# Exchanging the head of a fused attention and feed-forward kernel: single x tiles before the weights, chunk 0 in halves, dummy matmuls, V copied in one instruction

## Chip, cores and metric

One core of a Trainium2 chip runs the whole program. The time is device microseconds of one execution; lower is better. Five engines work side by side, each through its own instruction list in a fixed order: PE (matrix products), DVE (vector), ACT (scalar functions), POOL (general purpose) and SP, which here only starts transfers. An instruction that must wait for another engine or for a transfer holds up everything behind it on its own engine.

## What is computed

A transformer layer on x of 2048 rows (tokens) and 448 columns, bfloat16, cut to what matters:

```python
def layer(x):                       # x: 2048 x 448
    n = layernorm(x)
    q = n @ wq                      # 16 heads of 28
    k, v = n @ wk, n @ wv           # one head of 28, shared by all 16
    o = softmax(q @ k.T * 28**-0.5) @ v
    h = x + o @ wo
    n2 = layernorm(h)
    r = n2 @ w_r                    # pick the 8 best rows by r
    y = (silu(n2[idx] @ w_gate) * (n2[idx] @ w_up)) @ w_down * sigmoid(r[idx])
    return h + n2 + scatter(y, idx)
```

## The kernel before

**Tiles.** The 2048 tokens are 16 tiles of 128 (`t`, `j`), four of which make a chunk of 512. Attention runs in 16 blocks: block `b` is four heads (group `g = b % 4`) by the 512 queries of chunk `b // 4`. For each block and each of the 16 key tiles there are two products of Q with K (`qk`, one for each pair `p` of heads, into two banks of PSUM), an exponential of each on ACT (`act_unit`, L753, 128 x 1024 values), and four products with V that add up in bank 6 or 7 (`act_pv`). In blocks 1 to 15 three or four of the 16 key tiles go past ACT: `dve_unit` and `shift` build an approximate exponential on DVE out of integers (tile Y, L766 and L772, through PSUM banks 4 and 5, three Y buffers), and `dve_pv` multiplies its four shifted copies with four scaled copies of V. Block 0 has no such tile: all its 32 exponentials are ACT's.

**The head.** Before the first exponential there must be Q of block 0 and K of the first key tiles. `chunk(c)` makes K and V for 512 tokens: statistics (`bn_stats`, `bn_aggr`, L464 and L466) and normalisation (L479) of four tiles on DVE, rstd by Ln and Exp on ACT for chunk 0 and by a power on POOL for the others, transposes on PE, copies to `xnT` (L490 on ACT, L493 on DVE), the K product, K written twice with scale and offset (L501 on ACT, L505 on DVE), the V product, and five scaled copies of V (L516 on DVE). `q_project(b)` makes Q of a block (copied by L456). `wk_rep`, `wq_pad` and `wv_pad` are the weights spread out to 32 columns a head with zeros between, by POOL. All chunks but the first go through one PSUM bank, number 7 (`MISC`).

**Loads.** SP issues them in order: x tiles 0-1, 2-3, wk, wq, wv, the rest of x in fours, then w_r, the three feed-forward weights and wo.

**The order.** It isn't written out. Every operation is entered with its engine, its cost in ns, what it reads and writes, and a priority (lower first). `_Graph.plan` walks through time with these costs: an engine that is free takes, of the operations that are ready, the one of lowest priority, and ties go to the one entered first; if none is ready it takes the one that becomes ready next. After an operation its results count as ready only after `LAT` (190 ns PE, 110 ACT, 90 DVE, 120 POOL) and `SEM` (70 ns), after a transfer only after its `lat`. The order that comes out of this is fixed for each engine; on the chip, each engine follows it, however long things really take. Reading and writing a PSUM bank counts as using the key `pk(bank)`, so two operations on one bank run in the order in which they were entered. Events are entered by time: `chunk(c)` at 4c - 9, a tile of block b at 16b + j or so. So all chunks are entered before the first Y tile of block 1, which stands at 16.5.

Of the kernel before, what the change touches and what calls it, by code (L numbers as in the profile page):

```python
# [230 lines left out]
def _main(nc, G, sb, ps, psb, flag, scr, xs, A_x, A_wq, A_wk, A_wv, A_wo, B_w_r, B_w_gate, B_w_up, B_w_down, out,  # L231
          exact=False):
    S, D, H, C = A_x.shape[1], A_x.shape[2], 16, 8
    DH = D // H
# [10 lines left out]
    VC = (1.0, 1.6796875, 1.4140625, 1.1875, 1.0)  # L245
# [25 lines left out]
    vone = sb("vone", [128, NV, 4, 32], F32)  # L271
# [119 lines left out]
    G.op(PO, lambda e: e.memset(wk_rep[:, :, :], 0.0), 530, writes=["wk_rep"])  # L391
    for i in range(4):
        G.op(PO, lambda e, i=i: e.tensor_copy(wk_rep[0:CK, :, 32 * i:32 * i + DH], wk_sb[0:CK, :, :]), 300,
             reads=["wk_sb"], writes=["wk_rep"])
    G.op(PO, lambda e: e.memset(wq_pad[:, :, :, :], 0.0), 1800, writes=["wq_pad"])
    for ch in range(NCH):
        v = wq_pad[0:CK, ch, :, :].rearrange("p g (i c) -> p (g i) c", c=32)[:, :, 0:DH]
        G.op(PO, lambda e, ch=ch, v=v: e.tensor_copy(v, wq_sb[0:CK, ch, :].rearrange("p (h d) -> p h d", d=DH)), 590,
             reads=["wq_sb"], writes=["wq_pad"])
    G.op(PO, lambda e: e.memset(wv_pad[:, :, :], 0.0), 210, writes=["wv_pad"])  # L400
    G.op(PO, lambda e: e.tensor_copy(wv_pad[0:CK, :, 1:1 + DH], wv_sb[0:CK, :, :]), 280,
         reads=["wv_sb"], writes=["wv_pad"])
    G.op(PO, lambda e: e.memset(vone[:, :, :, :], 0.0), 500, writes=["vone"])
# [32 lines left out]
    G.op(DV, lambda e: e.memset(Lmx[:, :], 1.0), 90, writes=["Lmx"])  # L436
    G.op(DV, lambda e: e.tensor_reduce(sw[:, 0:1], w_rb[:, :], AX.X, ALU.add), dvt(D), reads=["w_rb"], writes=["sw"])
    G.op(DV, lambda e: e.tensor_scalar(sw[:, 1:2], sw[:, 0:1], -1.0, None, ALU.mult), 70, reads=["sw"], writes=["nsw"])

    head_banks = [7, 6, 5, 4, 3, 2, 1, 0]  # L440
    hb = [0]

    def head_bank(c):
        if c > 0:
            return MISC
        b = head_banks[hb[0] % len(head_banks)]
        hb[0] += 1
        return b
# [10 lines left out]
    def chunk(c):  # L459
# [48 lines left out]
        if c == 0:  # L508
            q_project(0, head_bank(c))
# [520 lines left out]
```

## Time and profile before

| | us |
|---|---|
| runs | 426.35, 428.45, 427.67 |
| median | 427.67 |
| profiled execution | 429.03 |
| its span, first to last instruction | 427.6 |

| engine | busy us | share | instructions |
|---|---|---|---|
| PE, products | 353.3 | 83% | 3243 |
| PE, weight loads | 106.0 | 25% | 3243 |
| DVE | 363.0 | 85% | 792 |
| ACT | 380.6 | 89% | 425 |
| POOL | 50.6 | 12% | 76 |

How to read the lines that follow. Engine rows of the 40 slices give the busy share in tenths, a slice being 10.7 us; PEclk is the granted clock of PE in tenths. The chain of waits gives the shares of the span on the way back from the last instruction. A group reads: line, engine, operation, written tile <- read tile, shapes, count | busy us in total, mean ns of one | idle us of the engine just before them and who ended it. In order of time a row reads: start, duration, engine, line, operation, count, and in brackets the idle time before it and what ended it. A windows row reads: from:to, length, then busy us and count for PE, its weight loads, DVE, ACT and POOL, granted clock, DMA share and GB/s (with one line of the kernel chosen, only the engine of that line has busy time). A row of DMA issues gives the count, the size of one in KB and the us from issue to landing. For a single tile a row gives duration in ns as least/median/most, and first and last start in us. SPq is SP's own instruction that issues a transfer.

### The profile page before, as it was taken

The page shows a single profiled execution, that of the slowest core. Times are in us where ns is not written, and L with a number is a line of the kernel's source. Part 1 is how long each engine was busy: PE and PEld are TensorE (multiplying, and loading weights), DVE is VectorE, ACT ScalarE, POOL GpSimd, SP SyncE. Part 2 cuts the span into 40 slices and gives each one's busy share as a digit, 9 for nine tenths or more (in the row PEclk, how much of TensorE's full clock was granted, in tenths as well). Part 3 has the DMA queues.
Part 4 walks back from the last instruction along what each step waited for, and adds up shares of the span by engine and source line. Part 5 has one row for each costly group of instructions (what it writes and reads, how often), then busy time and mean ns, then how long its engine had stood idle before and what let it go on. Part 6 is the DMA issues. An engine that isn't in the chain of part 4 may idle for free.

```text
span 427.6 us, 7935 instructions
## 1 busy us (share of the span) xinstructions
PE 353.3 (83%) x3243; PEld 106.0 (25%) x3243; DVE 363.0 (85%) x792; ACT 380.6 (89%) x425; POOL 50.6 (12%) x76
## 2 busy tenths in 40 slices
PE   0887898887888899789898897989898997898754
PEld 0333212221222222222222222222222222222243
DVE  4999819989897889989988999898989999998361
ACT  1397699999999999999999999999999999999640
POOL 8210000010010112010101030010101120313000
PEclk9998859999999999999999999999999999999965
DMA  8960000000000000200000001200000002000010
GB/s 225 266 206 19 2 2 28 2 27 2 26 3 20 10 17 12 90 25 3 27 2 26 4 25 53 63 0 26 6 27 2 18 10 91 27 2 27 2 44 8
DMA packets 17350, 15.75 MB, mean 37 GB/s; under 512 B 5944, under 2 KB 14428, under 8 KB 17308
## 3 DMA queue, kind: packets, MB, share of 16 engines
q1 hardware_dynamic: 17212, 15.16, 12.1%
q8 instruction: 27, 0.44, 0.4%
q14 instruction: 15, 0.12, 0.1%
q0 software_dynamic: 96, 0.02, 0.0%
HBM read 11.70 MB, written 3.47 MB: 35 GB/s over the span
## 4 chain that ended last, share of the span: by engine, by line
ACT 56%; PE 22%; DVE 18%; DMA 1%; issue 1%; SPq 1%; POOL 0%; POOLq 0%; DVEq 0%
ACT P L753 55%; PE ps L349 22%; DVE Y L766 5%; DVE Y L772 4%; DMA x_sb<-in_A_x_dram 1%; DVE xn L479 1%; DVE Ot L551 1%; DVE bn L464 1%; DVE K L505 1%; DVE xnT L493 1%; DVE Vs L516 1%; SPq L363 1%; DVE bn L687 1%; DVE junk L656 1%; DVE junk L664 0%
## 5 line engine op out<-in xcount | busy, mean ns | idle before, releaser
L753 ACT ACTIVATE P<-ps 128x1024 bf16<-128x1024 f32 x398 | 369.3, 1107 | 14.2 <-PE ps L349 12.8
L349 PE MATMUL ps<-Q,K 64*128 64x512 bf16 x1024 | 185.6, 391 | 44.0 <-ACT P L753 29.6
L766 DVE TENSOR_SCALAR Y<-ps 128x512 int16<-128x512 f32 x228 | 147.4, 682 | 18.0 <-PE ps L349 18.0
L772 DVE TENSOR_SCALAR Y<-Y 128x2048 int16<-128x2048 int16 x171 | 116.0, 710 | 1.4
L349 PEld LDWEIGHTS ps<-Q,K 64*128 64x128 bf16 x1024 | 44.7, 93 | 194.6 <-ACT P L753 156.1
L349 PE MATMUL ps<-P,Vs 128*32 128x512 bf16 x796 | 80.8, 396 | 0.3 <-ACT P L753 0.3
L349 PE MATMUL ps<-Y,Vs 128*32 128x512 bf16 x912 | 74.3, 383 | 0.0
L563 POOL TENSOR_TENSOR On<-Ot,Rb 128x512 bf16<-128x512 f32 x15 | 22.5, 1498 | 247.9 <-DMA Rb<-l_scr 247.9
L349 PEld LDWEIGHTS ps<-P,Vs 128*32 128x32 bf16 x796 | 20.5, 93 | 49.3 <-issue 48.3
L349 PEld LDWEIGHTS ps<-Y,Vs 128*32 128x32 bf16 x912 | 23.1, 96 | 18.4 <-issue 8.9
L349 PE MATMUL ps<-xnT,wq_pad 112*128 112x512 bf16 x64 | 21.8, 437 | 1.6 <-DVE Ot L551 1.3
L349 PE MATMUL ps<-wo_pad,On 128*128 128x448 bf16 (+1 forms) x64 | 17.8, 358 | 1.9 <-DVE Ot L551 1.1
L585 POOL TENSOR_TENSOR st<-st,nhalf 128x1 f32<-128x1 f32 x12 | 10.1, 841 | 65.8 <-DVE st L583 65.8
L456 DVE TENSOR_SCALAR Q<-ps,qone 128x512 bf16<-128x512 f32 x16 | 11.7, 732 | 7.0 <-PE ps L349 6.9
L551 DVE COPY Ot<-ps 128x512 f32<-128x512 f32 x15 | 10.3, 689 | 6.8 <-PE ps L349 6.1
L352 PE MATMUL ps<-ident,xn 128*112 128x128 bf16 x64 | 6.3, 259 | 11.2 <-POOL vone L405 10.5
L464 DVE BATCH_NORM_STATS2 bn<-x_sb 128x6 f32<-128x448 bf16 x16 | 9.4, 606 | 4.4 <-DMA x_sb<-in_A_x_dram 4.4
L579 DVE TENSOR_TENSOR hbuf<-ps,x_sb 128x448 f32<-128x448 f32 x12 | 7.5, 621 | 2.5 <-PE ps L349 2.5
L352 PEld LDWEIGHTS ps<-ident,xn 128*112 128x112 bf16 x64 | 5.2, 161 | 13.3 <-POOL vone L405 10.5
L598 DVE SCALAR_TENSOR_TENSOR junk<-hbuf,st,w_rb 128x448 bf16<-128x448 f32 x12 | 8.1, 678 | 0.0
L581 DVE BATCH_NORM_STATS2 bn<-hbuf 128x6 f32<-128x448 f32 x12 | 7.5, 622 | 0.1
L349 PEld LDWEIGHTS ps<-xnT,wq_pad 112*128 112x128 bf16 x64 | 4.4, 104 | 12.4 <-issue 8.1
(164 smaller groups left out, 156.7 us busy)
## 6 DMA issues: line engine op xcount, KB each, us to landing
Rb<-l_scr SPq DMA_DIRECT2D x15, 256.0 KB
wg_sb<-in_B_w_gate_dram SPq DMA_DIRECT2D x1, 1568.0 KB, 11.5
wu_sb<-in_B_w_up_dram SPq DMA_DIRECT2D x1, 1568.0 KB, 17.0
wd_sb<-in_B_w_down_dram SPq DMA_DIRECT2D x1, 1568.0 KB, 21.2
x_sb<-in_A_x_dram SPq DMA_DIRECT2D x3, 448.0 KB, 6.4
out_dram<-x_sb SPq DMA_DIRECT2D x3, 448.0 KB, 2.8
xn_scr<-xn SPq DMA_DIRECT2D x3, 448.0 KB, 3.8
x_sb<-in_A_x_dram SPq DMA_DIRECT2D x2, 224.0 KB, 2.8
```

Of the source, the lines that this page charges most:

```text
L349: return lambda e: e.matmul(o, lhsT=l, rhs=r, start=start, stop=stop)
L352: return lambda e: e.transpose(o, i, ident[0:p, 0:p])
L456: G.op(DV, lambda e: e.tensor_scalar(Q[:, b % 4, :], ps[:, bank, :], qone[:, 0:1], None, ALU.add), dvt(512), reads=[pk(bank), "qone"], wri ...
L464: G.op(DV, [lambda e, t=t: e.bn_stats(bn6[:, t, :], x_sb[:, t, 0:D])], dvt(D), reads=[("x", t)], writes=[("bn6", t)])
L551: G.op(DV, lambda e: e.tensor_copy(Ot[:, rb, :], ps[:, acc_bank(b), :]), dvt(512), reads=[pk(acc_bank(b))], writes=[("Ot", rb)], prio=u - 30)
L563: G.op(PO, lambda e: e.tensor_tensor(On[:, qb % 2, g, :], Ot[:, rb, :], Rb[:, rb, :], ALU.mult), 1270, reads=[("Ot", rb), ("Rb", rb)], wri ...
L579: G.op(DV, lambda e: e.tensor_tensor(hbuf[:, hr, :], ps[:, bank, 0:D], x_sb[:, t, 0:D], ALU.add), dvt(D), reads=[pk(bank), ("x", t)], writ ...
L585: G.op(PO, lambda e: e.tensor_tensor(st[:, t, 4:5], st[:, t, 7:8], nhalf[:, 0:1], ALU.pow), 570, reads=[("st7", t), "nhalf"], writes=[("st ...
L598: G.op(DV, lambda e: e.scalar_tensor_tensor(junk[:, :], hbuf[:, hr, :], st[:, t, 4:5], w_rb[:, :], ALU.mult, ALU.mult, accum_out=st[:, t, ...
L753: G.op(AC, lambda e: e.activation(P[:, sl, :, :], ps[:, b0:b0 + 2, :], ACT.Exp, bias=EBIAS, scale=OCT), 905, reads=[pk(b0), pk(b0 + 1)], w ...
L766: G.op(DV, lambda e, k=k: e.tensor_scalar(Y[:, n, 0, p + 2 * k, :].bitcast(I16), ps[:, 4 + k, :], 0.0, 32639.0 - 3 * STEP, ALU.max, ALU.mi ...
L772: G.op(DV, lambda e: e.tensor_scalar(Y[:, n, v, :, :].bitcast(I16), Y[:, n, 0, :, :].bitcast(I16), v * STEP, None, ALU.add), 610, reads=[( ...
```

## The change

- x tiles 0 to 3 are loaded one by one, then wk, wv, wq; the rest of x waits until tile 3 has landed; wo, w_r and the feed-forward weights wait until x tile 15 has landed. wo's four transfers no longer wait for one another.
- The weights are spread by ACT (`wk_rep` in one instruction, `wv_pad`, two of four pieces of `wq_pad`) and POOL (the other two). The zeros of `wk_rep` and `wv_pad` are written by DVE.
- Chunk 0 (`chunk0`, new): 44 dummy products of `ident` with itself into bank 7 first; rstd by halves of two tiles; transposes by tile into banks 0 to 3; the first half's `xnT` copied by ACT, the second's by DVE; K and Q of chunk 0 by halves of 256 tokens, K written by ACT; Q of the first half by ACT, of the second by DVE. Q of block 1 is entered at priority 9 instead of -100.
- Chunks 1 to 3: rstd of chunk 1 on ACT; five of twelve normalisations on POOL (with a negated mean, `nmean`); banks 7, 4, 5 in rotation in place of bank 7 alone. Statistics of a chunk wait for the last tile's statistics of the chunk before.
- V: the four scaled copies (five before, two of which had the scale 1.0) are written by one DVE instruction with a broadcast, and the column of constants is set once by POOL.
- `sw`, the sum over w_r, moves to priority 20.

```diff
-    VC = (1.0, 1.6796875, 1.4140625, 1.1875, 1.0)
+    VC = (1.0, 1.6796875, 1.4140625, 1.1875)
...
-    dma(x_sb[:, 0:2, 0:D], x_v[:, 0:2, :], [("x", t) for t in range(0, 2)], lat=2600.0)
-    dma(x_sb[:, 2:4, 0:D], x_v[:, 2:4, :], [("x", t) for t in range(2, 4)], lat=2600.0)
+    for t in range(4):
+        dma(x_sb[:, t, 0:D], x_v[:, t, :], [("x", t)], lat=2700.0 + 250 * t)
     dma(wk_sb[0:CK, :, :], A_wk.rearrange("(k p) n -> p k n", p=CK), ["wk_sb"], lat=4000.0)
-    dma(wq_sb[0:CK, :, :], A_wq.rearrange("(k p) n -> p k n", p=CK), ["wq_sb"], lat=6000.0)
-    dma(wv_sb[0:CK, :, :], A_wv.rearrange("(k p) n -> p k n", p=CK), ["wv_sb"], lat=6500.0)
+    dma(wv_sb[0:CK, :, :], A_wv.rearrange("(k p) n -> p k n", p=CK), ["wv_sb"], lat=4000.0)
+    dma(wq_sb[0:CK, :, :], A_wq.rearrange("(k p) n -> p k n", p=CK), ["wq_sb"], lat=5500.0)
     for i in range(4, NT, 4):
-        dma(x_sb[:, i:i + 4, 0:D], x_v[:, i:i + 4, :], [("x", t) for t in range(i, i + 4)], lat=6000.0)
+        dma(x_sb[:, i:i + 4, 0:D], x_v[:, i:i + 4, :], [("x", t) for t in range(i, i + 4)], lat=3500.0 + 400 * i,
+            reads=[("x", 3)])
...
+        if ch % 2:
+            G.op(AC, lambda e, v=v, w=w: e.activation(v, w, ACT.Identity), 480, reads=["wq_sb", "wq_pad"],
+                 writes=[("wq_pad", ch)])
+        else:
+            G.op(PO, lambda e, v=v, w=w: e.tensor_copy(v, w), 590, reads=["wq_sb", "wq_pad"],
+                 writes=[("wq_pad", ch)])
...
+    def v_project(c, bank):
+        pv = ps[:, bank, 0:128].rearrange("p (t c) -> p t c", c=32)
...
+        G.op(DV, lambda e: e.tensor_tensor(Vs[:, :, 4 * c:4 * c + 4, 1:32],
+                                           pv[:, :, 1:32].unsqueeze(1).broadcast_to([128, NV, 4, 31]),
+                                           vcc[:, :].unsqueeze(2).unsqueeze(3).broadcast_to([128, NV, 4, 31]),
+                                           ALU.mult), 620, reads=[pk(bank), "vcc"], writes=[("V", c)])
+
+    def chunk0():
+        G.prio = -500
+        for _ in range(44):
+            G.op(PE, mm(ps[:, 7, 0:128], ident[:, :], ident[:, :], True, True), 107, reads=["ident"], writes=[pk(7)],
+                 prio=-900)
...
+                G.op(AC, lambda e, sl=sl: e.activation(rstd[:, sl], var[:, sl], ACT.Exp, scale=-0.5), 200,
+                     reads=[("var", t // 2)], writes=[("rstd", -1 - t // 2)])
...
+            for kind in (("K", "Q") if h == 0 else ("Q", "K")):
+                bank = (4 if kind == "K" else 6) + h
...
+        v_project(0, 5)
+        G.prio = 9
+        q_project(1, MISC)
...
+        def head_bank():
+            hb[0] += 1
+            return (7, 4, 5)[hb[0] % 3]
...
-        for v in range(NV):
-            G.op(DV, lambda e, pv=pv, c=c, v=v: e.scalar_tensor_tensor(Vs[:, v, 4 * c:4 * c + 4, :], pv, VC[v],
-                                                                       vone[:, v, :, :], ALU.mult, ALU.add),
-                 dvt(128), reads=[pk(bank), "vone"], writes=[("V", c, v)])
+        v_project(c, head_bank())
...
-        G.op(PE, [mm(ps[32 * i:32 * i + 32, acc_bank(b), :], Vs[:, v + 1, j, :], Y[:, n, v, i, :], f, l)
+        G.op(PE, [mm(ps[32 * i:32 * i + 32, acc_bank(b), :], Vs[:, (v + 1) % NV, j, :], Y[:, n, v, i, :], f, l)
```

More of the change, by code (lines that the diff above doesn't have):

```diff
@@ L390, in _main @@
          writes=["qone"])
[L391 to L394, printed above, removed]
     G.op(PO, lambda e: e.memset(wq_pad[:, :, :, :], 0.0), 1800, writes=["wq_pad"])
+    G.op(DV, lambda e: e.memset(wk_rep[:, :, :], 0.0), 300, writes=["wk_rep"])
+    G.op(DV, lambda e: e.memset(wv_pad[:, :, :], 0.0), 100, writes=["wv_pad"])
@@ L400, in _main @@
[L400 to L403, printed above, removed]
+        w = wq_sb[0:CK, ch, :].rearrange("p (h d) -> p h d", d=DH)
+        if ch % 2:
[4 more added lines that the diff above has]
+                 writes=[("wq_pad", ch)])
@@ L577, in out_proj @@
                       for g in range(g2, g2 + 2)], 2 * 200,
-                 reads=[("On", qb % 2, g) for g in range(4)] + ["wo_pad"], writes=[pk(bank)])
+                 reads=[("On", qb % 2, g) for g in range(4)] + ["wo_pad"] + wok, writes=[pk(bank)])
         G.op(DV, lambda e: e.tensor_tensor(hbuf[:, hr, :], ps[:, bank, 0:D], x_sb[:, t, 0:D], ALU.add), dvt(D),
@@ L615, in first_top @@
         first_row(bank)
-    old = [("xnT", 0), ("xnT", 1)]
+    old = xk(0) + xk(1)
     def first_row(bank):
```

199 lines of the change are left out of this document (122 added, 77 removed).

## The prediction

> **What bounds the kernel now.** I read the page first: engine shares, the 40 slices, the chain of waits.
>
> ```profile
> span 427.6 us, 7935 instructions
> ACT  1397699999999999999999999999999999999640
> PEclk9998859999999999999999999999999999999965
> ACT P L753 55%; PE ps L349 22%; DVE Y L766 5%; DVE Y L772 4%; DMA x_sb<-in_A_x_dram 1%; DVE xn L479 1%; DVE Ot L551 1%; DVE bn L464 1%; DVE K L505 1%; DVE xnT L493 1%; DVE Vs L516 1%; SPq L363 1%; DVE bn L687 1%; DVE junk L656 1%; DVE junk L664 0%
> L753 ACT ACTIVATE P<-ps 128x1024 bf16<-128x1024 f32 x398 | 369.3, 1107 | 14.2 <-PE ps L349 12.8
> ```
>
> The 398 exponentials of L753 on ACT are the bound, except in the first six slices. So I split their time by windows, and listed ACT in order of time.
>
> ```profile
> 0.00:19.69 19.69, 0.00 (x0) 1.00 0.93 244
> 19.69:64.72 45.03, 35.74 (x37) 0.81 0.22 64
> 64.72:393.00 328.28, 326.80 (x355) 1.00 0.07 23
> 38.01 1.02 ACT L753 ACTIVATE P<-ps 128x1024 bf16<-128x1024 f32 x1 [2.11 <-PE ps L349]
> 48.97 1.02 ACT L753 ACTIVATE P<-ps 128x1024 bf16<-128x1024 f32 x1 [1.83 <-PE ps L349]
> 53.47 7.58 ACT L753 ACTIVATE P<-ps 128x1024 bf16<-128x1024 f32 x8 [1.32 <-PE ps L349]
> 61.85 2.12 ACT L753 ACTIVATE P<-ps 128x1024 bf16<-128x1024 f32 x2 [0.81 <-PE ps L349]
> 64.72 37.16 ACT L753 ACTIVATE P<-ps 128x1024 bf16<-128x1024 f32 x40 [0.75 <-PE ps L349]
> ```
>
> From 64.72 us on, 355 exponentials take 328.28 us, 0.925 each: nothing to win there, and the change leaves that part alone. The head loses twice. The first exponential starts at 19.69. The next 37 take 45.03 us where 37 x 0.925 = 34.2 would do: **10.8 us of waits**. The long ones, 2.11 and 1.83, are for the K of chunks 2 and 3 (16 keys of 128 make 32 exponentials per block; a chunk of K feeds 8).
>
> Why K is late, by engine:
>
> ```profile
> 20.00:51.00 31.00, 24.06 (x223) 9.85 (x221) 30.83 (x74) 24.67 (x26) 2.02 (x2) 0.93 0.30 90
> 51.00:63.50 12.50, 11.76 (x54) 2.23 (x54) 1.44 (x2) 10.29 (x12) 0.00 (x0) 0.50 0.01 1
> L766 DVE TENSOR_SCALAR Y<-ps 128x512 int16<-128x512 f32 x13 | 8.6, 687 | 3.3 <-PE ps L349 3.3
> L772 DVE TENSOR_SCALAR Y<-Y 128x2048 int16<-128x2048 int16 x9 | 6.0, 690 | 0.0
> 8.93 0.63 DVE L464 BATCH_NORM_STATS2 bn<-x_sb 128x6 f32<-128x448 bf16 x1 [2.69 <-DMA x_sb<-in_A_x_dram]
> ```
>
> DVE (third busy figure) is full for 31 us, then works 1.44 us of 12.5. In the full stretch it makes block 1's Y tiles (L766 and L772, 12 and 9 of the instructions) while ACT waits for chunks 2 and 3. The planner's fixed order let them in because all of chunks 1 to 3 pass through one bank. The last row is the same fault earlier: chunk 1's statistics were ordered ahead of chunk 0's normalisation, and DVE stood 2.69 us for their load.
>
> **The change, part by part.** The order on each engine follows from the costs in the diff; I walked `plan` through by hand for the head. Where an instruction stands comes from there, how long it lasts from rows.
>
> **First exponential.** It hangs on wq:
>
> ```profile
> 0.72 0.95 SPq L363 DMA_DIRECT2D x_sb<-in_A_x_dram  x2
> 2.23 0.48 SPq L363 DMA_DIRECT2D wq_sb<-in_A_wq_dram  x1
> 2.76 0.49 SPq L363 DMA_DIRECT2D wv_sb<-in_A_wv_dram  x1
> wq_sb<-in_A_wq_dram SPq DMA_DIRECT2D x1, 392.0 KB, 5.2
> L398 POOL COPY wq_pad<-wq_sb 112x448 bf16<-112x448 bf16 x4 | 2.3, 572 | 0.7 <-DMA wq_sb<-in_A_wq_dram 0.7
> 6.27 0.20 ACT L471 ACTIVATE var<-var 128x4 f32<-128x4 f32 x1 [4.27 <-DVE var L468]
> 11.66 1.02 ACT L490 ACTIVATE xnT<-ps 112x1024 bf16<-112x1024 bf16 x1 [4.95 <-PE ps L352]
> 15.53 0.78 ACT L501 ACTIVATE K<-ps,kb,ksc 128x512 bf16<-128x512 f32 x1 [2.85 <-PE ps L349]
> 13.62 1.86 PE L349 MATMUL ps<-xnT,wk_rep 112*128 112x512 bf16 x4 [1.15 <-DVE mv L466]
> 17.46 1.87 PE L349 MATMUL ps<-xnT,wq_pad 112*128 112x512 bf16 x4
> 19.26 0.75 PE L349 MATMUL ps<-Q,K 64*128 64x512 bf16 x4
> 25.09 1.04 PE L349 MATMUL ps<-xnT,wk_rep 112*128 112x512 bf16 x4
> ```
>
> wq lands at 2.23 + 5.2 = 7.4 now. Two more issues of x (0.48 each) and wv's (0.49) move ahead of its own: 1.45 later if issuing decides, about 0 if bytes do (25 KB more). I take 7.8, near the bytes, since its 5.2 us are mostly other data ahead of it. Bounds 7.4 to 8.9.
>
> In the plan wq is due at 5.92 and the second half's rstd (`Exp`) at 5.96, so on ACT two wq_pad copies stand ahead of that Exp and of the xnT copies; all of these wait in order for wq. From 7.8: two copies at 0.55 (POOL's 572 ns; ACT does not show them) make 8.9, Exp 0.2 makes 9.1, two half xnT at 0.6 (of 1.02) make 10.3. The K matmul of half 0 is half of 1.86 at the slow clock: 11.4 with its latency. Then ACT writes K twice and Q once at 0.45 (between 0.20 for 4 and 0.78 for 512): 12.8. PE meanwhile runs Q, Q, K of 0.85 each to 13.9, ACT writes the second K half, and the first exponential starts at **15.0**: 4.7 us earlier. ACT has nothing else to do before that; DVE's and POOL's chunk-0 steps end sooner and cost nothing. With PE fast the four half matmuls save 1.5.
>
> The rows show PE slow from 13.62 until the 0.75 at 19.26 (1.04 for the same four matmuls later), 5.6 us of steady work. The 44 dummies end near 6.6 (44 x 107 ns as the diff costs them); the gap to the first K matmul at 10.4 holds only transposes, so I take PE as slow. The Trainium skill, "TensorE: Matmul & The Clock Gate", Part 1 (The HAM clock gate), says that some 3.4 us of steady matmuls lift the gate and an idle window of 3.4 us brings it down. The row's 5.6 us is longer than its first figure; its second speaks against the dummies as placed, since their gap is 3.8 us. By lifting alone the estimate for the total would be 1.5 us lower; by both halves it is unchanged.
>
> **K of chunk 1.** Its matmul uses bank 7 after block 1's Q projection, whose DVE copy stands ahead of chunk 1's last `bn_aggr` (12.48 against 12.57 in the plan). Counting from Q's second half at 13.5 with the rows below: statistics and V to 15.6, Q of block 1 off PE at 17.0 and copied by 17.8, Ln and Exp between exponentials to 19.4, normalised at 20.4, transposed and copied at 22.2, K matmul 23.4, K at 24.2, exponential at 24.7. ACT is through with chunk 0 at 15.0 + 8 x 0.925 + 0.45 for Ln and Exp = 22.8: **a wait of 1.9**.
>
> ```profile
> L479 DVE TENSOR_SCALAR xn<-x_sb,mv,rstd 128x448 bf16<-128x448 bf16 x12 | 4.0, 394 | 0.0
> L493 DVE COPY xnT<-ps 112x1024 bf16<-112x1024 bf16 x6 | 4.1, 687 | 0.0
> L505 DVE TENSOR_SCALAR K<-ps,ksc,kb 128x512 bf16<-128x512 f32 x6 | 4.6, 802 | 0.0
> L579 DVE TENSOR_TENSOR hbuf<-ps,x_sb 128x448 f32<-128x448 f32 x12 | 7.5, 621 | 2.5 <-PE ps L349 2.5
> 49.85 1.08 DVE L516 SCALAR_TENSOR_TENSOR Vs<-ps,vone 128x128 bf16<-128x128 f32 x5
> L563 POOL TENSOR_TENSOR On<-Ot,Rb x15: 1267/1275/3502, 73.8 to 390.2; 128x512 bf16<-128x512 f32 x15
> ```
>
> **K of chunks 2 and 3.** Banks 7, 4, 5 now rotate, and Y uses 4 and 5. Y's instructions come later in the program, so no Y tile can start before chunk 3's K is written: DVE does chunks first. The V copy in one instruction of 496 elements is nearest to L579's 621 ns for 448; 0.6 for 1.08, 0.4 saved a chunk. Five normalisations go to POOL: bounds 0.57 (L398, one input) and 3.5 (longest of L563), taken 0.9. A mean of DVE's rows holds about 0.08 of overlap with the next instruction, so a chunk costs it four statistics at 0.6, two or three normalisations at 0.33, two copies at 0.6, two K at 0.72 and V's 0.6: some 6.5 us. Chunk 2's statistics are done while chunk 1 waits for POOL and PE, so after K1's second half at 25.0 come V, two normalisations, transposes and copies (1.9), K matmul (1.2) and K: K2 near 30, K3 one chunk later near 37. They are needed 8 x 0.925 = 7.4 apart, at 32.1 and 39.5: no wait. The Trainium skill, "GPSIMD Engine Reference", section 8 (Key points), has POOL share its SBUF interfaces with DVE; L563's spread of 1.27 to 3.50 agrees. At 3.5 each and 1.0 for each rstd, chunks 2 and 3 would cost POOL 16 us from 21 on, and with 2.7 for transposes, matmul and K the last K would come near 40, 0.5 late.
>
> **What stays.** Waits at 53.47, 61.85 and 64.72 fall in the stretch of clock 0.50; block 0 without Y's matmuls loads PE as lightly as then, so I keep all 2.88, 3.3 with a semaphore's hop each. The weights that now load after x have no reader before block 1 ends, and their 4.8 MB cross while no other load is due; without that cover the block's Rb loads would queue behind them. `sw`'s reduction moves behind the chunks into DVE's free time.
>
> **Sum.** 4.7 earlier; waits 0.45 + 1.9 + 3.3 = 5.65 instead of 10.8, 5.15 less; together 9.85. The profiled execution took 429.03 (span 427.6 and 1.4 around it): 419.2. The median shown, 427.67, lies 1.36 lower, so **417.8**.
>
> **Rivals.**
>
> 1. PE stays fast through chunk 0 and the late waits shrink too: first exponential at 13.5 and waits of about 3. 14 us, 413.7. For it: 25.09's speed and chunk work through 33 us; against: the gap after the dummies.
>
> 2. The waits come back: the order misses its loads as it did at 8.93, DVE stands for chunk 1, and all 10.8 stay. Only the earlier start counts, 4.7: 423.0. For it: wq is due at 5.92 in the plan and lands near 7.8; against: every late step is late by about the same 2 us.
>
> 3. Slower: PE holds its slow clock through block 0. These rows are the pattern:
>
> ```profile
> 56.00:58.00 2.00, 1.86 (x10) 0.32 (x8) 0.00 (x0) 2.00 (x3) 0.00 (x0) 0.50 0.00 0
> 41.09 1.10 PE L352 MATMUL ps<-ident,xn 128*112 128x128 bf16 x8
> 57.47 0.61 PE L349 MATMUL ps<-Q,K 64*128 64x512 bf16 x2
> ```
>
> At clock 0.50 the exponentials' own matmuls fill PE (1.86 of 2) and just feed ACT. Everything else then waits in ACT's time: three chunks of 2 x 1.10 + 1.86 + 0.6, three Q projections of 1.87, six Y products of 0.61, 23 us in all. With 0.45 that makes 12.65 more waits than the 10.8, less 4.7: 435.6. It decides from 15.5 us of waits on, two thirds of that work done slow. Against: PE came back to speed at 19.26 after 5.6 us of full work.
>
> 4. The head does not do what it says, nothing moves at the end: 427.7.
>
> **How the numbers follow.** Forecast 0.58, rival 1 0.15, rival 2 0.17, rival 3 0.07, rival 4 0.03. About 0.5% (2 us) is what a measurement here can tell from no change. Faster by more: 0.58 + 0.15 + 0.16 = 0.89; within: 0.04; slower: 0.07. The range runs from beyond rival 1 (wq at its early bound 7.4 on top, and its waits down by 0.8: 412.5) to just past rival 2 (423.5).
>
> **What would show it.** First exponential near 15.0; on ACT before it wq_pad copies waiting on wq's DMA near 7.8; no L766 before chunk 3's K; DVE's Q copy of block 1 ahead of `bn_aggr`; one wait of about 2 before the ninth exponential; the 40-exponential run starting near 55 instead of 64.72. It is wrong if the clock reads 0.50 for most of 20 to 45 us, if ACT waits more than 3 us for chunk 2 or 3, or if waits appear after block 1.

## The result, and the profile after

| | before | after |
|---|---|---|
| median, us | 428.06 (426.35 to 429.75, 4 runs) | 416.74 (415.54 to 417.05, 4 runs) |
| profiled execution, its span, us | 429.03, 427.6 | 416.59, 414.6 |
| first exponential starts, us | 19.69 | 15.02 |
| 38th exponential starts, us | 64.7 | 53.6 |
| waits between them, us | 10.8 | 4.4 |
| last exponential ends, us | 399.83 | 388.67 |

The ratio is 0.973 with an interval of 0.9686 to 0.9775: 11.3 us between the medians, where 9.85 were forecast. All of it is there by the 38th exponential (64.7 to 53.6, 11.1 earlier) and stays the same to the last one (11.16). In this table and below, the start of the 38th is the start of the run of exponentials in which it stands plus 0.925 for each one ahead of it in that run, and the waits are what is left of the way from the first to the 38th after 37 x 0.925 = 34.2. The traces' own start of the 38th lies within 0.4 of this figure.

The page after: span, the rows of ACT and of the granted clock in the 40 slices (10.4 us each now), and the group of exponentials.

```profile
span 414.6 us, 8038 instructions
ACT  4779999999999999999999999999999999999640
PEclk9799999999999999999999999999999999999955
L823 ACT ACTIVATE P<-ps 128x1024 bf16<-128x1024 f32 x398 | 368.5, 1116 | 5.1 <-PE ps L350 3.9
```

ACT is at 9 from the fourth slice on, where before it was from the sixth, and the granted clock has lost its dip (8, 8 and 5 in slices four to six); a 7 stands in the second slice, chunk 0's. The same 398 exponentials of the same length now stand idle 5.1 us in all, 14.2 before.

ACT in order of time:

```profile
7.74 1.04 ACT L405 ACTIVATE wq_pad<-wq_sb 112x448 bf16<-112x448 bf16 x2 [1.06 <-DMA wq_sb<-in_A_wq_dram]
...
8.78 1.06 ACT L501 ACTIVATE xnT<-ps 112x512 bf16<-112x512 bf16 x2
11.55 1.02 ACT L525 ACTIVATE K<-ps,kb,ksc 128x256 bf16<-128x256 f32 x2 [1.70 <-PE ps L350]
...
14.11 1.02 ACT L525 ACTIVATE K<-ps,kb,ksc 128x256 bf16<-128x256 f32 x2 [1.18 <-PE ps L350]
15.02 1.94 ACT L823 ACTIVATE P<-ps 128x1024 bf16<-128x1024 f32 x2
...
20.51 2.87 ACT L823 ACTIVATE P<-ps 128x1024 bf16<-128x1024 f32 x3 [0.53 <-PE ps L350]
25.14 4.93 ACT L823 ACTIVATE P<-ps 128x1024 bf16<-128x1024 f32 x5 [1.76 <-PE ps L350]
30.40 5.72 ACT L823 ACTIVATE P<-ps 128x1024 bf16<-128x1024 f32 x6 [0.34 <-PE ps L350]
36.55 2.86 ACT L823 ACTIVATE P<-ps 128x1024 bf16<-128x1024 f32 x3 [0.43 <-PE ps L350]
39.75 70.72 ACT L823 ACTIVATE P<-ps 128x1024 bf16<-128x1024 f32 x77 [0.34 <-PE ps L350]
```

The wait of 1.76 stands ahead of the ninth exponential: it is for chunk 1's K. Those for the K of chunks 2 and 3, 2.11 and 1.83 before, are gone, and so are the waits of 1.32, 0.81 and 0.75 at 53 to 65 us: from 39.75 on, 77 exponentials run without a listed stop, to the end of the view at 110 us.

DVE in order of time, the rows that tell the order:

```profile
21.38 0.72 DVE L463 TENSOR_SCALAR Q<-ps,qone 128x512 bf16<-128x512 f32 x1
...
23.86 1.51 DVE L588 TENSOR_SCALAR K<-ps,ksc,kb 128x512 bf16<-128x512 f32 x2
...
35.89 1.53 DVE L588 TENSOR_SCALAR K<-ps,ksc,kb 128x512 bf16<-128x512 f32 x2
...
38.53 1.29 DVE L836 TENSOR_SCALAR Y<-ps 128x512 int16<-128x512 f32 x2
```

The first Y tile starts after chunk 3's K, as forecast. Block 1's Q is copied at 21.38, much later than forecast: see below.

### The profile page after: what moved, and what is told of

Its sections match the earlier page's. It is cut to its first block, busy times and chain, and to the rows that moved or that the text cites. A ratio compares the mean times of both kernels' runs of the same rounds, so it can differ in the third digit from the quotient of the medians.

```text
span 414.6 us, 8038 instructions
## 1 busy us (share of the span) xinstructions
PE 349.3 (84%) x3295; PEld 110.5 (27%) x3295; DVE 359.5 (87%) x774; ACT 383.3 (92%) x438; POOL 49.5 (12%) x73
## 3 DMA queue, kind: packets, MB, share of 16 engines
q1 hardware_dynamic: 17244, 15.16, 13.3%
## 4 chain that ended last, share of the span: by engine, by line
ACT 62%; PE 21%; DVE 12%; DMA 2%; issue 1%; SPq 1%; POOL 0%; POOLq 0%; DVEq 0%; ACTq 0%
ACT P L823 62%; PE ps L350 21%; DVE Y L836 2%; DVE Y L842 1%; DVE K L588 1%; DVE Ot L621 1%; DMA wq_sb<-in_A_wq_dram 1%; DVE xnT L581 1%; DMA Lc<-l_scr 1%; SPq L364 1%; DVE bn L547 1%; DMA l_scr<-Ot 1%; DVE xn L565 1%; DVE junk L726 1%; DVE bn L757 1%
## 5 line engine op out<-in xcount | busy, mean ns | idle before, releaser
L350 PE MATMUL ps<-Q,K 64*128 64x512 bf16 x1024 | 182.7, 386 | 45.9 <-ACT P L823 32.3
L836 DVE TENSOR_SCALAR Y<-ps 128x512 int16<-128x512 f32 x228 | 147.2, 682 | 13.9 <-PE ps L350 13.8
L842 DVE TENSOR_SCALAR Y<-Y 128x2048 int16<-128x2048 int16 x171 | 114.7, 705 | 1.6
L350 PE MATMUL ps<-P,Vs 128*32 128x512 bf16 x796 | 79.3, 389 | 0.0
L633 POOL TENSOR_TENSOR On<-Ot,Rb 128x512 bf16<-128x512 f32 x15 | 21.4, 1429 | 239.4 <-DMA Rb<-l_scr 239.4
L350 PE MATMUL ps<-xnT,wq_pad 112*128 112x512 bf16 (+1 forms) x68 | 20.1, 393 | 0.6 <-DVE Ot L621 0.6
L350 PE MATMUL ps<-wo_pad,On 128*128 128x448 bf16 (+1 forms) x64 | 17.8, 358 | 2.3 <-DVE Ot L621 1.5
L621 DVE COPY Ot<-ps 128x512 f32<-128x512 f32 x15 | 10.3, 689 | 0.9 <-PE ps L350 0.3
L353 PE MATMUL ps<-ident,xn 128*112 128x128 bf16 x64 | 5.3, 236 | 3.1 <-DVE xn L493 2.7
L350 PEld LDWEIGHTS ps<-wo_pad,On 128*128 128x128 bf16 x64 | 4.2, 97 | 11.7 <-issue 6.9
L547 DVE BATCH_NORM_STATS2 bn<-x_sb 128x6 f32<-128x448 bf16 x12 | 6.9, 605 | 0.0
```

The source lines that it names most:

```text
L350: return lambda e: e.matmul(o, lhsT=l, rhs=r, start=start, stop=stop)
L547: G.op(DV, [lambda e, t=t: e.bn_stats(bn6[:, t, :], x_sb[:, t, 0:D])], 540, reads=[("x", t), ("mv", 4 * c - 1)], writes=[("bn6", t)])
L621: G.op(DV, lambda e: e.tensor_copy(Ot[:, rb, :], ps[:, acc_bank(b), :]), dvt(512), reads=[pk(acc_bank(b))], writes=[("Ot", rb)], prio=u - 30)
L633: G.op(PO, lambda e: e.tensor_tensor(On[:, qb % 2, g, :], Ot[:, rb, :], Rb[:, rb, :], ALU.mult), 1270, reads=[("Ot", rb), ("Rb", rb)], wri ...
L836: G.op(DV, lambda e, k=k: e.tensor_scalar(Y[:, n, 0, p + 2 * k, :].bitcast(I16), ps[:, 4 + k, :], 0.0, 32639.0 - 3 * STEP, ALU.max, ALU.mi ...
L842: G.op(DV, lambda e: e.tensor_scalar(Y[:, n, v, :, :].bitcast(I16), Y[:, n, 0, :, :].bitcast(I16), v * STEP, None, ALU.add), 610, reads=[( ...
```

## The experiments

The theory after the result: the gain has three sources that add up, the earlier first exponential, the bank rotation (chunks 1 to 3 ahead of the Y tiles), and a PE clock that no longer falls. The rivals: dummy products, POOL's normalisations or V's single instruction carry it; or it is the bank alone, or the order alone.

| run | first exponential | 38th | waits | median (range), us | ratio to before, 95% |
|---|---|---|---|---|---|
| e1_no_dummies | 15.00 | 53.5 | 4.3 | 416.52 (416.46 to 417.88) | 0.9655 to 0.9768 |
| e2_one_bank | 14.72 | 59.6 | 10.7 | 423.15 (421.91 to 424.83) | 0.9791 to 0.9918 |
| e3_before_rotate | 18.86 | 59.4 | 6.3 | 422.79 (421.31 to 423.51) | 0.9777 to 0.9894 |
| e4_wq_due | 12.93 | 50.6 | 3.4 | 413.00 (412.76 to 413.22) | 0.9565 to 0.9673 |
| e5_one_bank_hold | 15.16 | 56.4 | 7.1 | 420.63 (417.98 to 420.91) | 0.9722 to 0.9803 |
| e6_due_no_dummies | 13.75 | 51.4 | 3.4 | 414.46 (414.06 to 415.73) | 0.9619 to 0.9675 |
| e7_due_q1 | 13.61 | 53.1 | 5.3 | 416.62 (415.83 to 418.05) | 0.9657 to 0.9706 |
| e8_v_four | 14.98 | 53.9 | 4.7 | 416.47 (414.85 to 418.09) | 0.9689 to 0.9763 |
| e9_xn_dve | 14.59 | 52.2 | 3.4 | 415.69 (414.66 to 416.57) | 0.9677 to 0.9744 |
| e10_loads_free | 16.67 | 74.0 | 23.1 | 436.54 (435.47 to 437.70) | 1.0119 to 1.0185 |
| e11_due_v_late | 12.19 | 50.0 | 3.6 | 413.13 (412.22 to 413.81) | 0.9616 to 0.9680 |
| e12_due_xn_dve | 13.08 | 51.0 | 3.7 | 414.29 (412.99 to 415.67) | 0.9645 to 0.9735 |

The median of before beside them was 429.87 (e1 to e4), 429.72 (e5, e6, e7, e10), 427.97 (e8, e9, e11) and 427.99 (e12).

### The rotation of banks: undone, and alone

In the changed kernel, bank 7 alone again for chunks 1 to 3:

```diff
         def head_bank():
             hb[0] += 1
-            return (7, 4, 5)[hb[0] % 3]
+            return MISC
```

> The changed kernel with chunks 1 to 3 through bank 7 alone, as before. Theory: the bank rotation is what keeps block 1's Y tiles behind the chunks; with it gone the Y tiles stand among them in DVE's order again, ACT waits for K of chunks 2 and 3 (2 us or more each) and PE's clock may fall to 0.50 once more; the waits up to the 38th exponential grow from 4.3 to 8 to 11 us, 420.5 to 423.5. First exponential unchanged at 15.0. Rival: the waits shrank because DVE has less to do (POOL's normalisations, V in one instruction, ACT's share of chunk 0); then under 1.5 us is lost, 416.7 to 418.2.

In the kernel before, the rotation for chunks 1 to 3 and nothing else:

```diff
+    hc = [0]
...
-            return MISC
+            hc[0] += 1
+            return (7, 4, 5)[hc[0] % 3]
```

> The kernel before, with only the rotation of banks 7, 4, 5 for chunks 1 to 3 put in. Theory: first exponential stays at 19.7, no Y tile before chunk 3's K, the waits up to the 38th exponential fall from 10.8 to 4 to 6 us: 421.5 to 425. Rival: without the lighter DVE load of the new head K of chunks 2 and 3 is as late as before: no faster than 426.5.

ACT with one bank, in order of time:

```profile
27.86 1.02 ACT L823 ACTIVATE P<-ps 128x1024 bf16<-128x1024 f32 x1 [4.66 <-PE ps L350]
...
45.30 1.02 ACT L823 ACTIVATE P<-ps 128x1024 bf16<-128x1024 f32 x1 [0.61 <-PE ps L350]
46.78 1.94 ACT L823 ACTIVATE P<-ps 128x1024 bf16<-128x1024 f32 x2 [0.45 <-PE ps L350]
50.36 14.94 ACT L823 ACTIVATE P<-ps 128x1024 bf16<-128x1024 f32 x16 [1.65 <-PE ps L350]
```

and DVE in the same run:

```profile
25.99 0.66 DVE L836 TENSOR_SCALAR Y<-ps 128x512 int16<-128x512 f32 x1
26.57 1.52 DVE L588 TENSOR_SCALAR K<-ps,ksc,kb 128x512 bf16<-128x512 f32 x2
...
28.14 1.28 DVE L836 TENSOR_SCALAR Y<-ps 128x512 int16<-128x512 f32 x2
```

ACT in the kernel before with the rotation:

```profile
30.44 1.94 ACT L755 ACTIVATE P<-ps 128x1024 bf16<-128x1024 f32 x2 [2.14 <-PE ps L349]
...
42.72 37.69 ACT L755 ACTIVATE P<-ps 128x1024 bf16<-128x1024 f32 x41 [0.40 <-PE ps L349]
```

Without the rotation the waits are back at 10.7, those of before; with the rotation alone they fall to 6.3. The two halves nearly add up: by the 38th exponential the rotation alone gains 64.7 - 59.4 = 5.3 us, all the rest without it 64.7 - 59.6 = 5.1, together 10.4 of the 11.1. But 0.8 of the 5.3 is an earlier first exponential, which owes nothing to the rotation: in that profile DVE stood 2.09 us for chunk 1's load, 2.69 before, and the granted clock rose at 17.88, 19.26 before. The rotation's own share is the 4.5 by which the waits fall. By the medians of that session the halves are 7.1 and 6.7 (422.79 and 423.15 against 429.87), and the change without its dummies 13.35, so they add up there too. Against the expectation stands the place: the longest wait with one bank is 4.66 for chunk 1, not for chunks 2 and 3, and Y tiles (L836) stand on both sides of chunk 1's K. Also, with the rotation alone, 41 exponentials run from 42.72 without a listed stop: the waits at 53 to 65 us vanish without any other part of the change. PE's clock still fell in that profile, to 0.50 from 28.12 to 31.53 and once more at 96.39.

### Is it the bank or the order?

One bank, and Y held back behind chunk 3's K by one more read in `dve_unit`:

```diff
-        G.op(PE, qk(4, b, j, p), 216, reads=[("Q", b % 4), ("Qh", b % 4), kk(j, p)], writes=[pk(4), pk(5)], prio=t - 2.9,
+        G.op(PE, qk(4, b, j, p), 216, reads=[("Q", b % 4), ("Qh", b % 4), kk(j, p), ("K", 3, 1)], writes=[pk(4), pk(5)], prio=t - 2.9,
```

> Bank 7 alone for chunks 1 to 3, as in the run with one bank (423.15, waits of 10.6 us up to the 38th exponential, the longest 4.66 for chunk 1), and block 1's Y tiles now also wait for chunk 3's K. Theory A, the order is what costs: with one bank the Y tiles are placed between the chunks and take 15 DVE instructions (about 10 us) there, two of them ahead of chunk 1's K. Then without them the waits fall to 4 to 6 us and the time lies within 1 us of the changed kernel, 416 to 418. Theory B, the bank is what costs: transposes, K and V of a chunk have to follow one another through one bank, so the waits stay at 8 us or more and the time at 421 to 423.5. In both the longest DVE idle stretch moves behind chunk 3's K.

ACT in this run, in order of time:

```profile
27.72 1.03 ACT L823 ACTIVATE P<-ps 128x1024 bf16<-128x1024 f32 x1 [4.32 <-PE ps L350]
29.19 8.07 ACT L823 ACTIVATE P<-ps 128x1024 bf16<-128x1024 f32 x8 [0.45 <-PE ps L350]
37.45 7.64 ACT L823 ACTIVATE P<-ps 128x1024 bf16<-128x1024 f32 x8 [0.19 <-PE ps L350]
45.33 30.58 ACT L823 ACTIVATE P<-ps 128x1024 bf16<-128x1024 f32 x33 [0.25 <-PE ps L350]
```

Both theories miss: 7.1 us of waits lies between 4 to 6 and 8, and 420.63 between their ranges. It is both, each in its place. ACT's row for chunk 1 (4.32 after 4.66) hardly moves without Y tiles, so that wait is not theirs; it comes with the one bank, through which transposes, K and V of a chunk, and block 1's Q, go one behind another. The waits about chunk 3 fall with the Y tiles gone from among the chunks (0.61, 0.45 and 1.65 from 45 to 50 us, 0.25 left): those were the order's. Of the 6.0 us that the 38th exponential comes later with one bank than after the change, Y's place is 3.2 (59.6 - 56.4) and the bank 2.8 (56.4 - 53.6). The clock is in both figures: in the two profiles with one bank it read 0.50 while chunk 1 was made (20.33 to 23.74 and 21.26 to 24.67), which it did not after the change, and no run separates that.

### The dummy products

```diff
-        for _ in range(44):
+        for _ in range(0):
```

> The changed kernel without its 44 dummy matmuls. Theory: they lift PE's clock at about 5 us, it is down again at 8.8, and the K and Q matmuls of chunk 0 run at clock 0.50 anyway (10.3 to 15.5), so nothing is lost: first exponential at 15.0, time within 1 us of 416.7. Rival: the dummies pay; without them the transposes run slow too and PE is lifted later, first exponential 0.8 to 1.5 us later, 417.5 to 418.2.

First exponential 15.00 for 15.02, median 416.52 for 416.74: in the changed kernel the dummies are worth nothing. The K products of chunk 0 are as slow with them as without: ACT's waits for them are 1.70 and 1.10 us without, 1.70 and 1.18 with.

### A due time that fits the transfer

wq was planned to land at 5.92 us and landed at 7.7. Planned late enough, nothing of ACT's other work is ordered behind it:

```diff
-    dma(wq_sb[0:CK, :, :], A_wq.rearrange("(k p) n -> p k n", p=CK), ["wq_sb"], lat=5500.0)
+    dma(wq_sb[0:CK, :, :], A_wq.rearrange("(k p) n -> p k n", p=CK), ["wq_sb"], lat=7300.0)
```

> The changed kernel with wq's due time in the planner at 7300 ns instead of 5500 (it landed at 7.7). ACT's order then has the second rstd and the two xnT copies ahead of the wq_pad copies. Theory: the wait for wq no longer holds them; K of half 0 is made while wq lands, first exponential 1.5 to 2.5 us earlier, near 13.0; the wait for chunk 1's K grows by up to as much, since that chain hangs on DVE and x tiles 4 to 7 (landing at 9.8); total gain 0.5 to 2 us, 414.7 to 416.2. Rival: chunk 1's K decides alone, the start moves and the ninth exponential does not: 416.7, no gain.

ACT in this run, in order of time:

```profile
7.75 1.08 ACT L501 ACTIVATE xnT<-ps 112x512 bf16<-112x512 bf16 x2 [0.62 <-PE ps L353]
8.72 1.04 ACT L405 ACTIVATE wq_pad<-wq_sb 112x448 bf16<-112x448 bf16 x2
...
12.93 1.02 ACT L823 ACTIVATE P<-ps 128x1024 bf16<-128x1024 f32 x1 [0.98 <-PE ps L350]
...
22.16 4.87 ACT L823 ACTIVATE P<-ps 128x1024 bf16<-128x1024 f32 x5 [0.56 <-PE ps L350]
```

One number in the plan is worth 3.7 us here (416.74 to 413.00, ranges and intervals apart). xnT is copied ahead of wq_pad now, and the first exponential comes at 12.93 as expected. The gain is larger than expected because the chunk 1 chain moved too: the wait of 1.76 ahead of the ninth exponential is now 0.56, at 22.16. This is the fastest version of the study; nothing below went past it.

The same without the dummies:

```diff
-        for _ in range(44):
+        for _ in range(0):
```

> The version with wq's due time put at 7300 (413.0), without the 44 dummy products. Theory A, the dummies pay only where the gap after them is short: there PE made its first K product fast (1.05 us for eight), so without dummies chunk 0's products run at half speed, the first exponential moves from 12.93 to 13.9 to 14.8 and the time to 414 to 415. Theory B, the dummies are worth nothing here either and what sped PE up was the earlier start of its work: first exponential within 0.2 us of 12.93, time 412.6 to 413.4.

PE in order of time, without the dummies:

```profile
9.22 1.89 PE L350 MATMUL ps<-xnT,wk_rep 112*128 112x256 bf16 x8
10.90 1.34 PE L350 MATMUL ps<-xnT,wq_pad 112*128 112x256 bf16 x8
```

and with them, in the run above:

```profile
8.88 1.05 PE L350 MATMUL ps<-xnT,wk_rep 112*128 112x256 bf16 x8 [0.26 <-ACT xnT L501]
9.81 1.05 PE L350 MATMUL ps<-xnT,wq_pad 112*128 112x256 bf16 x8
```

Here the dummies pay: eight K products take 1.05 with them and 1.89 without, the first exponential moves by 0.82 and the median by 1.46 (the ranges are apart, the intervals of the ratios are not; the rows account for the 0.82). So part of the 3.7 us of the due time is the dummies' too. Whether dummies are worth anything hangs on what follows them.

### Three attempts to go further

Block 1's Q ahead of chunk 1, on the version with wq's due time:

```diff
-        G.prio = 9
+        G.prio = -100
         q_project(1, MISC)
```

> The version with wq's due time put at 7300 (413.0), with the Q projection of block 1 entered at priority -100 instead of 9, so that it leaves bank 7 before chunk 1's K needs it. Theory A, the late copy of block 1's Q is what chunk 1's remaining wait of 0.8 us is made of: the wait goes and the time is 412.0 to 412.7. Theory B, it only delays chunk 0's own second half by a copy of 0.72 us on DVE and a product of 0.94 us on PE: first exponential at 13.5 or later and time 413.2 to 414.

ACT in this run, in order of time:

```profile
13.21 0.21 ACT L552 ACTIVATE var<-mv 128x4 f32<-128x4 f32 x1 [1.45 <-DVE mv L549]
...
33.52 1.94 ACT L823 ACTIVATE P<-ps 128x1024 bf16<-128x1024 f32 x2 [1.37 <-PE ps L350]
```

The median is 3.6 us above that without it, several times what theory B gave, and by another way: the plan now puts chunk 1's Ln ahead of the first exponential on ACT, which holds ACT for 1.45 until DVE has the statistics, and longer waits follow at 26 to 36 us (0.84, 1.37, 0.62), with the granted clock at 0.50 from 30.52 to 33.94. As Ln moved along with it, the run does not show what an earlier Q of block 1 is worth by itself.

V's product of chunk 0 behind the first products of Q and K, on the same version:

```diff
-             reads=["wv_pad"] + xk(c), writes=[pk(bank)])
+             reads=["wv_pad"] + xk(c) + ([] if c else [("Qh", 0)]), writes=[pk(bank)])
...
+        G.prio = 0
         v_project(0, 5)
```

> The version with wq's due time put at 7300 (413.0), with V's product of chunk 0 behind the first two products of Q and K instead of ahead of them. There V's product waited 1.14 us on bank 5 for ACT's second K half at 11.99 and the first product of Q and K followed at 12.49. Theory A, this wait stands on the path of the first exponential: Q's second half is written at 11.4, the first exponential moves from 12.93 to 11.8 to 12.1, and the time to 411.9 to 412.4. Theory B, the start moves but chunk 1's K is then waited for by as much (its wait of 0.8 us grows to 1.6 to 1.8): 412.7 to 413.3.

ACT in this run, late in its order of time:

```profile
156.73 228.79 ACT L824 ACTIVATE P<-ps 128x1024 bf16<-128x1024 f32 x246 [0.65 <-PE ps L350]
```

The first exponential moves to 12.19, a little less than expected, the 38th is 0.6 earlier, but the time is the same, 413.13. Neither theory: chunk 1 takes nothing back. In this profile a wait of 0.65 stands at 156 us, where the version it was made from has none, and eats the gain. PE stood 1.06 us for one of DVE's Y tiles just before; why in this run and not in the other was not settled.

The normalisations on DVE again, alone:

```diff
-            if t % 2 == 0 or t == 7:
+            if True:
```

> The changed kernel with all twelve normalisations of chunks 1 to 3 on DVE instead of five of them on POOL (0.72 to 0.82 us each there, about 0.33 on DVE). Theory A, POOL takes work off a full DVE: two of DVE's slots of 0.33 come back into chunks 2 and 3 each and one into chunk 1, small waits of 0.3 to 0.7 more on ACT, time 417 to 418. Theory B, POOL is the slower way: its hop and its 0.8 us stand in chunk 1's chain, whose wait of 1.76 us shrinks by 0.2 to 0.6, time 415.8 to 416.5.

and on the version with wq's due time:

> Both edits that helped in one kernel: wq's due time at 7300 (413.0) and all normalisations of chunks 1 to 3 on DVE (alone 415.69 against 416.74). Theory A, they add up: the run without waits starts as much earlier again as it did alone (1.3 us at the 38th exponential), time 411.6 to 412.4, first exponential near 12.9. Theory B, in the run with the normalisations on DVE the gain came from the first exponential alone (14.59 for 15.02), in which PE's clock came back sooner; here PE is not slow at that point, so nothing is added: time 412.6 to 413.4.

Alone, 415.69 with a range that overlaps the changed kernel's: the normalisations on POOL bring nothing that shows. The 38th exponential comes 1.4 us earlier, against theory A, but not by theory B's way: chunk 1's wait stays at 1.82, and the first exponential gains 0.43. That 0.43 can be the clock's: in this profile it rose at 13.09, after the change at 15.53, and chunk 0's second K product took 0.66 instead of 1.06. On the version with wq's due time nothing is added (414.29, range 412.99 to 415.67); theory A falls, and theory B's time is missed by 0.9.

### V in one instruction, and the late loads

```diff
-        G.op(DV, lambda e: e.tensor_tensor(Vs[:, :, 4 * c:4 * c + 4, 1:32],
...
+        for v in range(NV):
+            G.op(DV, lambda e, v=v: e.tensor_scalar(Vs[:, v, 4 * c:4 * c + 4, 1:32], pv[:, :, 1:32], VC[v], None,
+                                                    ALU.mult), dvt(128), reads=[pk(bank)],
```

> The changed kernel with V's four scaled copies written by four DVE instructions of 128 x 124 values instead of one of 128 x 496. Five such took 1.08 us before, one copy now takes 0.65 to 0.68, so DVE has 0.2 to 0.4 us more work in each of four chunks. Theory A, DVE's chunk work sets chunk 1's start and some of this lands on ACT: the 38th exponential 0.2 to 1 us later, time 416.9 to 417.8. Theory B, DVE waits elsewhere by as much and nothing lands: within 0.3 us of 416.7.

Four instructions took 0.84 to 0.87 where one takes 0.65 to 0.68. The time is 416.47: theory B, no difference that can be told.

The later loads let go:

```diff
-        dma(x_sb[:, i:i + 4, 0:D], x_v[:, i:i + 4, :], [("x", t) for t in range(i, i + 4)], lat=3500.0 + 400 * i,
-            reads=[("x", 3)])
+        dma(x_sb[:, i:i + 4, 0:D], x_v[:, i:i + 4, :], [("x", t) for t in range(i, i + 4)], lat=3500.0 + 400 * i)
...
-    dma(w_rb[:, :], B_w_r.partition_broadcast(128), ["w_rb"], reads=[("x", NT - 1)], lat=6000.0)
+    dma(w_rb[:, :], B_w_r.partition_broadcast(128), ["w_rb"], lat=6000.0)
```

(and so for wo and the three feed-forward weights).

> The changed kernel with the later loads let go: the rest of x no longer waits for tile 3, and wo, w_r and the feed-forward weights no longer wait for x tile 15. Theory A, holding them back matters only for the first 8 us, in which the wait for wq takes part: the 16 transfer engines then share more bytes, wq lands 0.5 to 3 us later than 7.7, the first exponential moves by as much from 15.0, and the time is 417 to 420. Theory B, transfers are served in the order of issue and wq stands ahead of all of them, so nothing moves: first exponential 14.9 to 15.1, time 416 to 417.3.

SP's issue of wo in this run:

```profile
9.24 17.88 SPq L364 DMA_DIRECT2D wo_pad<-in_A_wo_dram  x4
```

and DVE, in order of time:

```profile
8.96 0.63 DVE L546 BATCH_NORM_STATS2 bn<-x_sb 128x6 f32<-128x448 bf16 x1 [3.54 <-DMA x_sb<-in_A_x_dram]
...
33.78 0.63 DVE L725 SCALAR_TENSOR_TENSOR junk<-wo_pad,w_rb 128x448 bf16<-128x448 bf16 x1 [18.28 <-DMA wo_pad<-in_A_wo_dram]
```

Neither theory, and some 20 us slower than the changed kernel. wq is not the point: ACT's copy of it starts at 7.91 instead of 7.74. But SP issues wo last here, behind the feed-forward weights, and takes 17.88 us over it (1.65 after the change, where wo goes ahead of them), while the plan believes in 6 us and has put the sum over wo on DVE right behind chunk 1's statistics, ahead of its normalisation. DVE stands 18.28 us at it, and ACT with it. Earlier it stands 3.54 us for chunk 1's x ahead of chunk 0's normalisation, the fault of before (2.69) again. As the edit changes SP's order too, it does not show what holding back costs or gains alone; it shows what an instruction ordered ahead of a late transfer costs.

## Why the prediction was right, and where it was not

**First exponential, 15.0 against 15.02.** Right in its main steps: ACT's copy of wq starts at 7.74 (7.8 forecast), the two wq_pad copies stand ahead of xnT on ACT, and PE is slow through chunk 0. The hundredths are luck. ACT was through with both xnT copies at 9.85, not 10.3, but PE started the first K product only behind the second half's transposes, which hung on the Exp that wq held up:

```profile
9.55 1.10 PE L353 MATMUL ps<-ident,xn 128*112 128x128 bf16 x8 [1.75 <-DVE xn L493]
10.45 1.06 PE L350 MATMUL ps<-xnT,wk_rep 112*128 112x256 bf16 x4
```

The run with another due time shows that wq's place in the order holds the start back to 15.0. Which parts of the new head brought it forward from 19.69 is not shown: no run takes the halves, the order of the loads or the spreading by ACT out again. The rows divide the 4.67 only in part. Chunk 0's normalisations end at 11.01 before and at 9.80 after, 1.2 us; and before, PE made block 1's Q (from 17.46) ahead of the first product of Q with K at 19.26, though block 0's Q had been copied by 17.98, by estimate 1.2 us more.

**Chunk 1's K, a wait of 1.9 against 1.76.** The size came out by errors that cancel. The prediction put DVE's copy of block 1's Q ahead of chunk 1's last `bn_aggr`, at 17.0 to 17.8; it stands behind chunk 1's xnT copies, at 21.38 to 22.10, and the K product, which needs the same bank 7, starts at 22.24. The Q is entered at priority 9, behind all three chunks (-3, 1 and 5). Against that, Ln and Exp were through at 18.15 instead of 19.4, and the xnT copies at 21.36 instead of 22.2. Chunk 1's K is written from 23.86 on, and the ninth exponential is at 25.14 for 24.7; ACT was through with chunk 0 at 23.38 for 22.8, so the wait is nearly the same. The sign for this step, named at the prediction's end, did not show.

**Chunks 2 and 3, no wait.** Right: 0.34, 0.43 and 0.34 are left there, and their K is written from 30.22 and 35.89 on (forecast near 30 and 37). That the Y tiles stand behind chunk 3's K was forecast; the runs with one bank show that this order is worth 3.2 us, and the free banks as such another 2.8, the clock's part included.

**The late waits, 3.3 kept, none seen.** This is the term that was mis-sized. The prediction took the slow clock at 50 to 63 us as the consequence of a lightly loaded block 0, which would stay. The chance that it would go was given to rival 1, but there it was tied to a fast PE in chunk 0, which did not come. The runs show it tied to the order that the rotation brings: with the rotation alone the 41 exponentials from 42.72 have no listed stop, and with one bank but Y held back the 33 from 45.33 have none either. In place of the 3.3 stand small waits of 0.53, 0.34, 0.43 and 0.34, 1.64 in all. With 1.76 for chunk 1 and 0.42 for Ln and Exp that is 3.8 of the 4.4; the rest is not in a listed wait. Forecast were 5.65.

How the slow clock came and went, by windows of 3.41 us, before:

```profile
12.43:15.85 3.42, 2.27 (x7) 0.86 (x7) 2.93 (x10) 0.57 (x2) 1.40 (x3) 1.00 1.04 263
15.85:19.26 3.41, 3.41 (x24) 1.17 (x24) 2.84 (x8) 0.45 (x1) 0.00 (x0) 1.00 1.04 269
...
46.57:49.98 3.41, 2.08 (x28) 0.78 (x26) 3.35 (x6) 1.58 (x2) 0.00 (x0) 1.00 0.00 0
49.98:53.39 3.41, 3.06 (x12) 0.67 (x10) 1.42 (x6) 1.95 (x3) 0.00 (x0) 0.50 0.00 0
...
63.63:67.05 3.42, 3.42 (x32) 0.84 (x28) 2.96 (x8) 2.67 (x4) 0.00 (x0) 1.00 0.04 7
```

and after:

```profile
1.87:5.29 3.42, 3.42 (x33) 3.42 (x34) 2.46 (x8) 0.13 (x1) 3.42 (x7) 1.00 0.79 152
5.29:8.70 3.41, 1.52 (x21) 1.19 (x19) 0.82 (x3) 2.23 (x8) 1.70 (x11) 1.00 1.01 300
8.70:12.11 3.41, 2.56 (x16) 2.12 (x17) 2.73 (x6) 1.71 (x6) 1.74 (x12) 0.50 0.68 213
12.11:15.53 3.42, 3.42 (x16) 1.48 (x14) 2.31 (x10) 2.25 (x6) 0.00 (x0) 0.50 0.66 147
...
36.01:39.42 3.41, 2.98 (x29) 1.03 (x25) 3.41 (x8) 2.97 (x4) 0.00 (x0) 1.00 0.00 1
...
42.83:46.25 3.42, 2.26 (x18) 0.59 (x16) 3.42 (x6) 3.42 (x5) 0.00 (x0) 1.00 0.00 0
```

Before, PE (first busy figure) waited for chunk 3's K and was busy 2.08 of 3.41; the next window began at half speed, and it took 13.65 us to come back. After, the window in which chunk 3's K is made has 2.98, and the next three have 2.63, 2.26 and 2.30. With one bank, where Y tiles stand among the chunks again, the window with chunk 3's K has 2.08 and half speed follows, from 47.63 to 51.05. That the clock stays up because the K waits no longer empty PE fits these windows, and the late waits go in both runs that keep Y behind the chunks. It is not shown by itself: after the change a window with 2.20 (22.35 to 25.76) was followed by no drop, and before one with 2.22 was.

The windows also explain the dummies. They fill the window to 5.29, and PE is lifted there. In the next one PE has 1.52, and it is slow again from 8.70 until the full window to 15.53 is over: the prediction's choice, with the reason that it gave, the gap behind the dummies. It is not the phase of one execution alone. In four profiles with this order (after the change, with one bank, with four V instructions, with all normalisations on DVE) the window behind the lift has 1.52, 1.20, 1.62 and 1.10, and a drop follows each time; in the four with wq's due time and dummies it has 2.72, 2.75, 2.04 and 1.83, and none follows. In a further one (one bank, Y held back) the dummies did not lift PE at all: they filled 2.75 of the window to 7.60, and the clock rose only at 14.43.

**V, POOL, Ln and Exp.** V took 0.65 to 0.68 (0.6), POOL's normalisations 0.72 to 0.82 (0.9), Ln and Exp 0.42 (0.45). The first two do not decide: the time is the same with four V instructions and with all normalisations on DVE. The bound of 3.5 for POOL was far off; the longest normalisation on POOL in any of the profiles is 1.58, in the two with one bank, and its cause is not shown.

**Sum.** 4.67 of the 4.7 for the first exponential; waits down by 6.4 where 5.15 were forecast; together 11.1 for 9.85. The median came out at 416.74 for 417.8, 1.1 lower, and the 1.3 us of waits account for that. Of the three sources in the theory above, the runs show the order and the banks, and that the earlier start comes without them (14.72 with one bank); the clock's share lies within their figures and is not separated.

## What to carry to other kernels

Where the order is planned from costs, a due time that is earlier than the transfer lands puts other work behind it on an engine that runs its list in order: compare each due time with the landing in the trace first (one of them was worth 3.7 us here, and one instruction ordered ahead of a late transfer cost 18). In this plan, two chains that share a PSUM bank run in the order of entry, and what is free of it overtakes them; look at what the engine does while the bottleneck waits, as with DVE's Y tiles here. Dummy products pay only if real products follow at once: count PE's busy time in the 3.41 us window behind them (1.10 to 1.62 was too little here, 1.83 to 2.75 enough), not their number.

## What the runs showed of the hardware

**PE's clock changes on a grid.** In all fourteen profiles the changes of the granted clock lie whole multiples of 3.41 us apart, with another phase in each execution: slow from 39.74 to 43.16 and from 49.98 to 63.63 before (3.42 and 4 x 3.41, the starts 3 x 3.41 apart), from 8.70 to 15.53 after (2 x 3.41), from 28.12 to 31.53 in the kernel before with the rotation. Counted back on the same grid, the edge at 19.26 in the rows of before is where PE's products became fast: a full window (15.85 to 19.26) had passed, while the 5.6 us that the prediction counted began inside the window ahead of it. The Trainium skill, "TensorE: Matmul & The Clock Gate", Part 1 (The HAM clock gate), says that the activity window is free-running and 3413 ns long, and that the transition therefore moves with the phase; the traces agree, with 3.41. It also says that a window without work brings the clock down. Here less is enough: leaving out the run with the loads let go and the end of each kernel, there are fourteen drops, and in the window before each PE was busy between 1.10 and 2.22 of the 3.41 us. It isn't the whole rule, though: other windows, from 1.80 (the run with V's product late, from 155.05) to 2.22, were followed by none, and of the slow windows one with 3.06 and one with 3.16 ended the slow stretch and others with 3.06 and 3.14 didn't. Some matmul records can be missing, so these sums are not exact.

**A granted clock of 1.00 early in a profile can be untrue.** Without the dummies the record reads 1.00 from the start, yet K's first product in chunk 0 takes 1.06 us, as long as with it at 0.50, and before it reads 1.00 at 12.43 to 19.26 while four products take 1.86 us and later 1.04. In each trace the first entry of the clock is its first change; what the views give ahead of that is not a measurement.
